# Retention, ELU layer and max-out layer on one core: the planner's stores become steps of their own, ring loads are cut in pieces, buffers change their homes

## The chip, the cores and the metric

The kernel runs on 1 core of a Trainium2 chip. The metric is the device time of one execution in microseconds, lower is better; a program is run several times and the median is given. One further execution was recorded by the profiler; all rows below come from it.

The engines are named as the profile names them: PE is TensorE's matmul, PEld its weight load, DVE VectorE, ACT ScalarE, POOL GpSimd, SP SyncE, which here only issues DMAs. A DMA issue can stand on SP, ACT or POOL, and each of these works through its instructions in the order of the program.

## What is computed

Three stages in a row, all in float32; the weights of stages two and three are stored as float64.

```python
# 1: retention; q, k, v are (4, 8, 768, 64), one decay gamma for each head
for t in range(S):
    state = gamma * state + outer(k[:, :, t], v[:, :, t])
    y[:, :, t] = scale * (q[:, :, t] @ state)
x = y.transpose(0, 2, 1, 3).reshape(3072, 512)
# 2: 512 -> 2048 -> 512 with ELU
h = x @ w_in
x = where(h > 0, h, exp(min(h, 0)) - 1) @ w_out
# 3: 512 -> 768 -> 512, the largest of three products
h = maximum(maximum(x @ w1, x @ w2), x @ w3)
out = h @ w_out2
```

## The kernel before

Float32 values are split into a high and a low part, and three products (high-high, high-low, low-high) stand for one. A matmul has 128 rows, 128 columns and 512 moving columns.

**Stages of work.** The 3072 tokens are six blocks of 512 (`b` 0 to 5). Retention goes by 24 chunks of 128 tokens (`c`), each with scores, a mask, an update of the state and value products. The first chunks and the first products of blocks 0 and 1 are ordered by a list of names (`FIRST`). Then follows the planned part. For blocks 0 to 3 and each of the 16 slices `f` of the inner width there is a first product (`h1_products`, 12 matmuls), the ELU on ACT and DVE (`elu_exp`, `elu_max`, `elu_high`, `elu_low`) and a second product (`o1`, 12 matmuls) that adds into four PSUM banks. Between them stand visits to later chunks (`TURNS` says at which slices). Blocks 4 and 5 are taken together in eight units of seven products of six matmuls (`unit_a`): the operands are sums of quarters of the input and of the weight, so seven products do for eight. The third stage, behind the planned part, uses units of the same kind (`unit`) in a written order.

**Preparation.** The weights of the units are made on the way. `prepare_first` (8 jobs) makes the seven operands of a unit from the split weights of stage two and stores them to `ops_a` in DRAM; `prepare` (12 jobs, `JOBS`; nine with three pairs, three with two) reads float64 words, turns them to float32 in steps on ACT and DVE, forms sums and splits them, and stores the parts to `ops_d`. They use small rings of SBUF buffers: `t` (2), `m` (2), `st` (2 raw words). `prepare_some` adds job `k` to the plan when `(i - BEGIN) * RATE` has passed it, where `i` counts iterations. Where it is added sets which turn in the rings it gets; the planner then decides when it runs.

**The units' ring.** Stored operands come back to SBUF through a ring of three 1 MB buffers of four operands each (`ring`, `fetch`, issued on POOL). A buffer is asked for again when its last operand has been used.

**The planner.** `Plan.add` takes an engine, a cost, a function, and tokens that it reads, writes or comes after. `turn` hands out ring buffers as tokens. `latest` works back from the order of TensorE's steps to the time by which each step is due. `run` plays the plan with the costs: each engine takes, of the steps that are ready, the one that is due first; TensorE may take one of the next six. The functions are then called in the order of the starting times, so each engine's program has that order, and at run time it is kept whatever is late. A store is issued by the function of the step that ends its data (`store`, `store_a`), and a step on the pretended engine Q (`later_read`) holds the buffer for the length of the move. All moves share one queue in the model.

**Partial sums.** `sums_out` and `x2_out` copy the four PSUM banks of a block to SBUF, two on ACT (to `m` buffers) and two on DVE (to `e` buffers, which the ELU uses too), and store them to `x2d`: from ACT's queue, or from POOL's with an addition in DRAM (`again`). Chunks 16 to 23 are stored to `xd` from ACT's queue (`finish_copies`, a buffer of their own, `late_x`). `load_x2("a")` reads `xd` back for the units, and `first_operands` makes the operands of it.

Of the kernel before, what the change touches and what calls it, by code (L numbers as in the profile page):

```python
# [38 lines left out]
TURNS = ((1, 3, 5, 7, 9, 11, 13, 15), (1, 3, 5, 7))  # L39
BEGIN, RATE = 18, 0.31  # L40
# [24 lines left out]
def kernel(ctx: ExitStack, tc: tile.TileContext, qkv0, qkv, wa, wb, dmask, qdec, cols, out):  # L65
# [23 lines left out]
    late_x = ctx.enter_context(tc.tile_pool(name="late_x", bufs=1))  # L89
# [202 lines left out]
    def finish_copies(c):  # L292
        if c >= DEFER:
            x, t0 = late_x.tile([P, NPAIR, P], F32, tag="x", name="xf"), (c - DEFER) * P
            for s in range(2):
                nc.scalar.copy(x[:, :, s * HC:(s + 1) * HC], xo_t[c][s])
            nc.scalar.dma_start(out=xd.rearrange("k p t -> p k t")[:, :, t0:t0 + P], in_=x)
            return
        xh, xl = x_t[c // CB]
        t0 = c * P % BLK  # L300
        xo = xo_t[c]
        for s in range(2):
            nc.scalar.copy(xh[:, :, t0 + s * HC:t0 + (s + 1) * HC], xo[s])

# [236 lines left out]
    def x2_out(b, ms=range(KDM), again=False):  # L541
        for m in ms:
            if b == NB - 1:
                o = (
                    states.rearrange("p b n d -> p (b n d)")[:, m // 2 * BLK:(m // 2 + 1) * BLK] if m % 2 == 0
                    else at.tile([P, BLK], F32, tag=("a", "qd")[m // 2], name="o")
                )
            elif m % 2 == 0:
                o = dpool.tile([P, BLK], F32, tag="m", name="o")
            else:  # L550
                o = gpool.tile([P, BLK], F32, tag="e", name="o", bufs=3)
            to = x2d[m, :, b * BLK:(b + 1) * BLK]
            if m % 2 == 0:
                nc.scalar.copy(o, acc_t[b][m])  # L554
            else:
                nc.vector.tensor_copy(o, acc_t[b][m])
            if again:
                nc.gpsimd.dma_start(out=to, in_=o, accum_op=ALU.add)
            else:
                nc.scalar.dma_start(out=to, in_=o)  # L560
# [4 lines left out]
    class Plan:  # L565
        LAG = {"P": 0.2, "A": 0.06, "D": 0.06, "G": 0.06, "S": 0.06, "Q": 0.0}

        REACH = 6
        FREE = {"P": 0.0, "A": 1.8, "D": 1.4, "G": 0.0, "S": 0.0, "Q": 0.0}
# [4 lines left out]
        def add(self, engine, cost, fn, reads=(), writes=(), after=(), pair=False, move=0.0):  # L574
# [13 lines left out]
            lag = self.LAG[engine] + (move + 3.0 if move else 0.0)  # L588
            self.steps.append((engine, cost, fn, sorted(deps), pair, lag, move))
            return k  # L590

        def turn(self, ring, size):
            n = self.count[ring] = self.count.get(ring, -1) + 1
            return (ring, n), (ring, n - size)

        def latest(self):
# [8 lines left out]
            for _ in range(3):  # L605
                for k in reversed(range(n)):
                    engine, cost, _, _, _, lag, _ = self.steps[k]
                    if engine != "P":
                        ends = [due[u] - lag for u in users[k]]
                        if due[k] is not None:  # L610
                            ends.append(due[k] + cost)
                        due[k] = min(ends, default=clock) - cost
                for engine in "ADG":
                    line = sorted((k for k in range(n) if self.steps[k][0] == engine), key=lambda k: -due[k])
                    end = clock
                    for k in line:
                        due[k] = min(due[k], end - self.steps[k][1])
                        end = due[k]
            return due, users

        def run(self):
            n, due = len(self.steps), None
            due, users = self.latest()
            left, at = [len(x[3]) for x in self.steps], [0.0] * n
# [3 lines left out]
            start, late = [None] * n, 0.0  # L628
            port, queue = [0.0, None], [0.0]
# [4 lines left out]

            def begin(k, t):
                engine, cost, _, _, pair, lag, move = self.steps[k]
                if move:
                    queue[0] = max(queue[0], t + cost + 0.65) + move
                    lag = queue[0] - t - cost + 0.75
# [8 lines left out]
                for u in users[k]:  # L648
                    own = engine == self.steps[u][0] and engine in "P"
                    at[u] = max(at[u], t + cost + (0.0 if own else lag))  # L650
                    left[u] -= 1
                    if not left[u]:
                        known[self.steps[u][0]].append(u)
                        heapq.heappush(times, at[u])

            while len(order) < n:
                assert times, [(k, self.steps[k][0]) for k in range(n) if start[k] is None][:20]
                t = heapq.heappop(times)
                while times and times[0] <= t + 1e-6:
                    heapq.heappop(times)  # L660
                busy = True
                while busy:
                    busy = False
                    for engine in "PSQGAD":
# [11 lines left out]
                        soon = [k for k in known[engine] if at[k] > t + 1e-6]  # L676
                        for k in sorted((k for k in known[engine] if at[k] <= t + 1e-6), key=lambda k: (due[k], k)):
                            end = t + self.steps[k][1]
# [29 lines left out]
    def later_read(*tokens, move=0.77):  # L708
        plan.add("Q", 0.5, None, reads=tokens, writes=(), move=move)

    def prepare_first(p):
# [6 lines left out]
        def whole(i):  # L718
            def fn():
# [3 lines left out]
                for j, n in ((0, 0), (1, 3)) if i == 0 else ((1, 5),):  # L723
                    store_a(slot + n, w[:, :, j * HB:(j + 1) * HB])
# [8 lines left out]
        def third_high():  # L733
            third[0] = dpool.tile([P, 2, HB], F32R, tag="m", name="m")
            nc.scalar.copy(third[0][:, 0], b12())

        def third_low():
            m = third[0]
            nc.vector.tensor_tensor(out=m[:, 1], in0=b12(), in1=f32(m[:, 0]), op=ALU.subtract)
            store_a(slot + 4, m)  # L740
# [4 lines left out]
        def last_low():  # L745
            x = b22()
            nc.vector.tensor_tensor(out=x.bitcast(F32R), in0=x, in1=b12(), op=ALU.subtract)
            store_a(slot + 1, f32(t[1]).rearrange("p (s t) -> p s t", s=2))

        def combined_high():  # L750
            third[1], third[2] = [dpool.tile([P, 2, HB], F32R, tag="m", name="m") for _ in range(2)]
            nc.scalar.copy(third[1], f32(t[0]).rearrange("p (s t) -> p s t", s=2))

        def combined_low():
# [4 lines left out]
            for part, m in enumerate((hi, lo)):  # L759
                stored_a.update((slot + n, part) for n in (2, 6))  # L760
                nc.sync.dma_start(out=ops_a[:, slot + 2:slot + 7:4, part, :], in_=f32(m))

        wait = [("hi", 4 * p), ("lo", 4 * p), ("hi", 4 * p + 2), ("lo", 4 * p + 2)]
        (m0, n0), (m1, n1), (m2, n2) = short("m", 2), short("m", 2), short("m", 2)
# [5 lines left out]
        later_read(wt, ("t", t0), move=1.54)  # L770
        later_read(wt, ("t", t1))
# [6 lines left out]
        plan.add("Q", 0.5, None, [m0], [("prep", p, 0)], move=0.77)  # L778
        add("A", 0.62, combined_high, [A, B_], [m1], [n1, n2])
        add("D", 0.69, combined_low, [A, B_, m1], [m2, t0], [A], True)  # L780
        plan.add("Q", 0.5, None, [m1, m2], [("prep", p, 1)], move=1.54)
        add("A", 0.41, last_high, [D_], [C_])
        add("D", 0.42, last_low, [C_], [D_, t1], (), True)
        plan.add("Q", 0.5, None, [t1, wt], [("prep", p, 2)], move=0.77)

    def prepared(n):
        return [("prep", p, j) for p in sorted({(4 * n + i) // 7 for i in range(4)}) for j in range(3)]

    def prepare(k, slot):
# [20 lines left out]
        def words(i):  # L810
# [27 lines left out]
            add("S", 0.5, load, (), [r], [r0], move=1.54)  # L838
# [5 lines left out]
        def parts(i, key, put):  # L844
            (x, x0), (y, y0) = short("m", 2), short("m", 2)

            def high():
                made[key] = [dpool.tile([P, 512], F32R, tag="m", name="m") for _ in range(2)]
# [177 lines left out]
    def fetch_step(n, reads=(), after=()):  # L1026
        def fn():
            fetch(n)
# [720 lines left out]
```

## Time and profile before

| | us |
|---|---|
| median of 3 runs | 963.96 |
| lowest and highest | 962.66, 966.68 |
| the profiled execution | 970.78 |
| its span, from the first to the last instruction | 968.9 |

The page of the profile gives the busy time of each engine, the chain of work that ended last, and the costliest groups of instructions. A busy time counts an instruction from its start to its end. An idle time is put down to the instruction or DMA that ended it. The stretches that matter here: the list `FIRST` until about 115 us, the planned part until 606 us, and stage three to the end.

### The profile page before, as it was taken

The page shows a single profiled execution, that of the slowest core. Times are in us where ns is not written, and L with a number is a line of the kernel's source. Part 1 is how long each engine was busy: PE and PEld are TensorE (multiplying, and loading weights), DVE is VectorE, ACT ScalarE, POOL GpSimd, SP SyncE. Part 2 cuts the span into 40 slices and gives each one's busy share as a digit, 9 for nine tenths or more (in the row PEclk, how much of TensorE's full clock was granted, in tenths as well). Part 3 has the DMA queues.
Part 4 walks back from the last instruction along what each step waited for, and adds up shares of the span by engine and source line. Part 5 has one row for each costly group of instructions (what it writes and reads, how often), then busy time and mean ns, then how long its engine had stood idle before and what let it go on. Part 6 is the DMA issues. An engine that isn't in the chain of part 4 may idle for free.

```text
span 968.9 us, 16300 instructions
## 1 busy us (share of the span) xinstructions
PE 941.3 (97%) x6583; PEld 770.4 (80%) x6583; DVE 636.4 (66%) x1047; ACT 369.2 (38%) x669; POOL 112.5 (12%) x146
## 2 busy tenths in 40 slices
PE   6999989999999999999998999999999999999998
PEld 4778878877878878887876888888888888888886
DVE  6888678566663346698876888478744787346651
ACT  3566555334443344575654564121220213101111
POOL 2510010214212222000000000100000010000000
PEclk9999999999999999999998999999999999999999
DMA  9934454668763378737776864866525654245602
GB/s 312 327 103 162 136 169 148 144 200 227 229 181 105 110 250 280 235 118 264 242 254 221 280 226 153 303 218 189 191 87 217 194 198 162 98 145 191 206 1 87
DMA packets 86347, 183.26 MB, mean 189 GB/s; under 512 B 6400, under 2 KB 51712, under 8 KB 78336
## 3 DMA queue, kind: packets, MB, share of 16 engines
q1 hardware_dynamic: 67776, 103.83, 32.6%
q0 software_dynamic: 10672, 69.48, 22.6%
q10 hardware_dynamic: 7824, 8.92, 2.7%
q8 instruction: 52, 0.85, 0.4%
q14 instruction: 23, 0.19, 0.1%
HBM read 131.08 MB, written 51.12 MB: 188 GB/s over the span
## 4 chain that ended last, share of the span: by engine, by line
PE 84%; DMA 7%; DVE 4%; ACT 2%; issue 1%; SPq 1%; ACTq 0%; POOL 0%; DVEq 0%; POOLq 0%
PE hp L1163 26%; PE acc L536 18%; PE hp L485 11%; PE acc L1223 10%; PE acc L472 6%; PE hp L462 5%; PE hp L1079 4%; DMA ops_d<-m 2%; DMA ops_a<-t 1%; PE xs L263 1%; PE acc L1163 1%; PE xs L252 1%; PE xs L222 1%; PE xs L194 1%; DMA x<-in_qkv 1%
## 5 line engine op out<-in xcount | busy, mean ns | idle before, releaser
L1163 PE MATMUL hp<-seat,w 128*128 128x512 f32 x1092 | 249.2, 390 | 0.0
L1163 PEld LDWEIGHTS hp<-seat,w 128*128 128x128 f32 x1092 | 204.7, 188 | 43.6 <-ACT states L554 0.4
L536 PE MATMUL acc<-gh,w 128*128 128x512 f32 x600 | 155.9, 399 | 8.5 <-ACT gh L518 8.5
L536 PEld LDWEIGHTS acc<-gh,w 128*128 128x128 f32 x600 | 112.8, 191 | 34.2 <-ACT gh L518 10.2
L485 PE MATMUL hp<-xh,w 128*128 128x512 f32 x376 | 123.7, 390 | 0.0
L1223 PE MATMUL acc<-w,g 128*128 128x512 f32 x432 | 99.1, 389 | 0.0
L1223 PEld LDWEIGHTS acc<-w,g 128*128 128x128 f32 x432 | 81.1, 188 | 16.8
L1079 PE MATMUL hp<-seat,w 128*128 128x512 f32 x336 | 79.7, 395 | 5.3 <-DVE hold L1097 4.6
L536 PE MATMUL acc<-gl,w 128*128 128x512 f32 x300 | 83.8, 393 | 0.4 <-issue 0.4
L485 PEld LDWEIGHTS hp<-xh,w 128*128 128x128 f32 x376 | 70.6, 188 | 14.8
L1079 PEld LDWEIGHTS hp<-seat,w 128*128 128x128 f32 x336 | 63.6, 190 | 19.9 <-DVE hold L1097 5.7
L510 DVE SCALAR_TENSOR_TENSOR e<-e,hp 128x512 f32<-128x512 f32 x59 | 40.5, 686 | 58.1 <-ACT e L504 57.6
L485 PE MATMUL hp<-xl,w 128*128 128x512 f32 x188 | 73.2, 389 | 0.0
L1189 ACT COPY u<-hp 128x512 f32<-128x512 f32 x26 | 15.3, 587 | 138.3 <-PE hp L1163 138.3
L536 PEld LDWEIGHTS acc<-gl,w 128*128 128x128 f32 x300 | 56.7, 190 | 12.8 <-issue 0.8
L503 ACT ACTIVATE e<-hp 128x512 f32<-128x512 f32 x59 | 35.2, 596 | 82.7 <-PE hp L485 68.0
L931 POOL DMA_DIRECT2D w<-ops_d x48 | 25.4, 529 | 355.5 <-PE hp L1163 278.7
L522 DVE TENSOR_TENSOR gl<-e,gh 128x512 fp32r<-128x512 f32 x75 | 53.2, 709 | 14.5 <-ACT gh L518 13.1
L518 ACT CAST gh<-e 128x512 fp32r<-128x512 f32 x75 | 46.4, 619 | 37.4 <-DVE e L510 28.8
L472 PE MATMUL acc<-gh,w 128*128 128x512 f32 x168 | 44.1, 392 | 0.4 <-ACT gh L518 0.4
L171 POOL TENSOR_TENSOR x<-x,cols_sb 128x512 f32<-128x512 f32 x24 | 27.4, 1145 | 137.3 <-DMA x<-in_qkv 137.3
L1180 ACT CAST g<-e 128x512 fp32r<-128x512 f32 x36 | 22.2, 623 | 52.2 <-DVE e L1177 51.8
(146 smaller groups left out, 1294.1 us busy)
## 6 DMA issues: line engine op xcount, KB each, us to landing
w<-ops_d POOLq DMA_DIRECT2D x48, 1024.0 KB, 5.1
x<-in_qkv SPq DMA_DIRECT2D x44, 512.0 KB, 6.4
ops_d<-m SPq DMA_DIRECT2D x66, 256.0 KB, 3.7
raw<-in_wa SPq DMA_DIRECT2D x32, 512.0 KB, 6.1
w<-ops_a POOLq DMA_DIRECT2D x14, 1024.0 KB, 6.8
raw<-in_wb SPq DMA_DIRECT2D x24, 512.0 KB, 4.4
ops_a<-w SPq DMA_DIRECT2D x24, 256.0 KB, 5.2
ops_a<-m SPq DMA_DIRECT2D x24, 256.0 KB, 3.8
```

What stands on the lines that cost most here:

```text
L171: nc.gpsimd.tensor_tensor(out=kd, in0=kd, in1=cols_sb[:, 0:H].rearrange("t (p r) -> t p r", r=2).unsqueeze(3).to_broadcast([P, NPAIR, 2, D ...
L462: nc.tensor.matmul(hp_t[b, f], w_t[0, f // 2][:, f % 2, pw, kk * P:(kk + 1) * P], x_t[b][px][:, kk, :], start=i == 0 and kk == 0, stop=i = ...
L472: nc.tensor.matmul(acc_t[b][m], w_t[1, f // 2][:, f % 2, pw, m * P:(m + 1) * P], g_t[b, f][pg], start=f == f0 and i == 0, stop=f == f1 - 1 ...
L485: nc.tensor.matmul(hp, w[:, pw, kk * P:(kk + 1) * P], x[px][:, kk, :], start=k == 0, stop=k == len(order) - 1,)
L503: nc.scalar.activation(e, hp_t[b, f], ACTF.Exp)
L510: nc.vector.scalar_tensor_tensor(out=e, in0=e, scalar=-1.0, in1=hp_t.pop((b, f)), op0=ALU.mult, op1=ALU.max)
L518: nc.scalar.copy(gh, e_t[b, f])
L522: nc.vector.tensor_tensor(out=gl, in0=e_t.pop((b, f)), in1=f32(gh), op=ALU.subtract)
L536: nc.tensor.matmul(acc_t[b][m], w[:, p[0], m * P:(m + 1) * P], g[p[1]], start=f == f0 and p == first, stop=f == f1 - 1 and p == final, ski ...
L1079: nc.tensor.matmul(ps[name], w[:, pw, kk * P:(kk + 1) * P], x[px][:, kk, :], start=first and k == 0, stop=last and k == 5, skip_group_chec ...
L1163: nc.tensor.matmul(o, w[:, pw, kk * P:(kk + 1) * P], x[px][:, kk, :], start=first and k == 0, stop=last and k == 5, skip_group_check=True,)
L1223: nc.tensor.matmul(acc, g2[f][:, px, m * P:(m + 1) * P], w[:, pw, :], start=f == 0 and i == 0, stop=f == KF2 - 1 and i == 2, skip_group_ch ...
```

## The change

Constants: `TURNS` moves five of twelve visits by one slice, `RATE` goes from 0.31 to 0.5, `OPERANDS` says after which slices of block 3 the steps of `first_operands` are added (all at slice 14 before). The pool `late_x` goes, `m` has three buffers. In the planner, a store is a step on S (SP) or G (POOL); its move is a count and a time of pieces; the two queues are played side by side. A step after a DMA that isn't urgent waits a margin longer, and an issue that isn't due soon is kept back while its queue is full. The visits of chunks 8 to 11 are placed one iteration earlier and the hand-written case of the last of them goes.

```diff
-TURNS = ((1, 3, 5, 7, 9, 11, 13, 15), (1, 3, 5, 7))
-BEGIN, RATE = 18, 0.31
+TURNS = ((1, 3, 5, 7, 9, 11, 13, 14), (2, 4, 6, 8))
+BEGIN, RATE = 18, 0.5
+OPERANDS = (10, 11, 11, 12, 14, 14, 14)
...
-            x, t0 = late_x.tile([P, NPAIR, P], F32, tag="x", name="xf"), (c - DEFER) * P
+            x, t0 = gpool.tile([P, NPAIR, P], F32, tag="e", name="xf", bufs=3), (c - DEFER) * P
...
-            nc.scalar.dma_start(out=xd.rearrange("k p t -> p k t")[:, :, t0:t0 + P], in_=x)
+            late_t[c] = x, xd.rearrange("k p t -> p k t")[:, :, t0:t0 + P]
...
+    def store_late(c):
+        x, to = late_t.pop(c)
+        nc.sync.dma_start(out=to, in_=x)
...
+        elif b < 2 and m % 2 == 0:
+            o = dpool.tile([P, BLK], F32, tag="m", name="o", bufs=3)
+        elif b == NB - 3 and m % 2 == 0:
+            o = at.tile([P, BLK], F32, tag=("a", "qd")[m // 2], name="o")
+        else:
+            o = gpool.tile([P, BLK], F32, tag="e", name="o", bufs=3)
...
+    def x2_store(b, m, o, again=False, eng=nc.sync):
...
+        SLOW = (1.1, 1.5, 1.0, 1.0, 12.0)
...
+        def lag(self, k):
+            engine, cost, _, _, _, move = self.steps[k]
+            return self.LAG[engine] + (3.5 + move[0] * move[1] if move else 0.0)
...
+            def done(k, when, margin):
+                for u in users[k]:
+                    at[u], safe[u] = max(at[u], when(u)), max(safe[u], when(u) + margin)
...
+            def carried(t):
+                while True:
+                    heads = [x[0] for x in lanes.values() if x]
+                    cut = min(t, arrivals[0][0]) if arrivals else t
+                    if heads:
+                        turn = sum(x[2] for x in heads) * self.SLOW[0]
+                        least = min(x[1] for x in heads)
...
+                                        done(x.pop(0)[0], lambda u: clock[0] + 0.75, self.SLOW[1])
...
+                    x = t + (0.8 if engine == "S" else 1.4)
...
+                            if safe[k] > t + 1e-6 and due[k] + late > t + self.SLOW[2]:
+                                continue
+                            if full and self.steps[k][5] and due[k] + late > t + self.SLOW[4]:
+                                continue
...
-    def later_read(*tokens, move=0.77):
-        plan.add("Q", 0.5, None, reads=tokens, writes=(), move=move)
...
+        def put(reads, fn, *made):
+            add("S", 0.42, fn, reads, [("op", slot + n, part) for n, part in made], move=(16, 0.047))
...
-            (x, x0), (y, y0) = short("m", 2), short("m", 2)
+            (x, x0), (y, y0) = short("m", 3), short("m", 3)
...
-                for part, m in enumerate(made[key]):
-                    put(part, m)
...
+            for part, z in enumerate((x, y)):
+                add(
+                    "S", 0.42, lambda part=part: put(part, made[key][part]), [z], [("there", slot, key, part)],
+                    move=(16, 0.047),
+                )
...
-    def fetch_step(n, reads=(), after=()):
+    def fetch_step(n, i, reads=(), after=()):
+        plan.add(
+            "G", 0.6, lambda: fetch(n, i), reads, [("ring", n, i)], list(after) + [("ring", n - RING, i)],
+            move=(10, 0.098),
+        )
...
-            add("S", 0.9, lambda: load(c), (), [raw_of(c)], [raw_of(c - 2)], move=3.1)
+            before = [raw_of(c - 2), kv_of(c - 2)]
+            add("S", 0.42, lambda: load(c, "qk"), (), [raw_of(c)], before, move=(21, 0.098))
+            add("S", 0.42, lambda: load(c, "kv"), (), [kv_of(c)], before, move=(44, 0.052))
...
-            x, x0 = plan.turn("late", 1)
+            x, x0, _ = e_ring()
...
-    for k in range(KF2 // 2):
-        fetch_out(k)
...
+                if x == 0 and 2 <= n < 2 + KF2 // 2:
+                    fetch_out(n - 2)
```

## Rows read from the trace of the kernel before

**Rows 1.** The page, busy time, share of the span, instructions of TensorE.

```profile
PE 941.3 (97%) x6583; PEld 770.4 (80%) x6583; DVE 636.4 (66%) x1047; ACT 369.2 (38%) x669; POOL 112.5 (12%) x146
```

**Rows 2.** Busy time by stage, the planned part: length, engines (count), clock, DMA share, GB/s.

```profile
115.00:606.00 491.00, 476.31 (x3950) 390.23 (x3949) 335.58 (x580) 241.32 (x450) 64.83 (x72) 0.99 0.64 203
```

**Rows 3.** Whom TensorE waited for, 115 to 606 us: total, times, longest.

```profile
PE acc L536 <- ACT gh L518: 8.5, 4, 2.6
PE hp L1079 <- DVE hold L1097: 4.6, 2, 3.6
PE hp L1079 <- DVE e L1042: 0.7, 1, 0.7
```

**Rows 4.** The chain that ended last, pieces in order of time: start, length, what.

```profile
196.46 2.72 PE acc L536 x12
...
202.30 6.29 DMA ops_a<-t
...
211.47 4.61 PE acc L536 x12
...
489.18 8.77 DMA ops_d<-m
...
520.60 2.93 PE hp L1079 x6
523.53 6.79 PE acc L536 x24
```

**Rows 5.** Busy time by stage, behind the last of these waits.

```profile
520.00:540.00 20.00, 19.40 (x74) 15.86 (x75) 14.56 (x26) 8.47 (x15) 1.06 (x2) 0.85 0.62 201
```

**Rows 6.** DMA issues (KB each, median us to landing), and the `ops_d` stores of line 699.

```profile
ops_a<-t SPq DMA_DIRECT2D x8, 256.0 KB, 5.7
...
DMA to landing us min/median/max: 1.7/3.4/8.8
```

**Rows 7.** Busy time by stage of line 852 alone; the timeline of ACT.

```profile
230.00:341.00 111.00, 0.00 (x0) 1.00 0.53 153
341.00:448.00 107.00, 10.34 (x14) 1.00 0.69 225
...
340.54 0.58 ACT L554 COPY o<-acc 128x512 f32<-128x512 f32 x1
```

**Rows 8.** Busy time by stage: PE, PEld, DVE, ACT, POOL, clock, DMA share, GB/s.

```profile
230.00:448.00 218.00, 215.19 (x2356) 176.59 (x2355) 134.26 (x238) 103.78 (x206) 38.74 (x41) 1.00 0.61 188
285.00:341.00 56.00, 56.00 (x738) 46.21 (x742) 21.18 (x40) 20.23 (x44) 11.62 (x12) 1.00 0.37 109
```

**Rows 9.** DVE by line, 135 to 610 us: count, busy us, mean ns, idle before.

```profile
L852 DVE TENSOR_TENSOR m<-t,m 128x512 fp32r<-128x512 f32 x33 | 23.4, 710 | 15.3 <-DMA ops_d<-m 8.5 <-ACT m L849 6.6
L833 DVE SCALAR_TENSOR_TENSOR t<-raw,t 128x512 uint32<-128x512 uint32 x24 | 16.5, 690 | 0.2
...
L808 DVE TENSOR_TENSOR t<-t 128x256 f32<-128x256 f32 x36 | 15.2, 421 | 0.7
```

**Rows 10.** SP's waits, 110 to 140 us; the chain there.

```profile
SPq L122 <- DMA x2d<-o: 8.9, 1, 8.9
...
124.83 7.17 DMA raw<-in_wa
```

**Rows 11.** The ring's loads (line 931): us from issue to landing.

```profile
DMA to landing us min/median/max: 4.4/5.2/10.3
```

**Rows 12.** The timelines of DVE and of POOL at 121 us.

```profile
121.39 1.53 DVE L433 TENSOR_TENSOR w<-t,w 128x512 fp32r<-128x512 f32 x1
...
120.89 1.48 POOL L171 TENSOR_TENSOR x<-x,cols_sb 128x512 f32<-128x512 f32 x1 [63.78 <-DMA x<-in_qkv]
```

**Rows 13.** The timelines of POOL (a chunk's keys) and of TensorE (its scores).

```profile
296.36 1.04 POOL L171 TENSOR_TENSOR x<-x,cols_sb 128x512 f32<-128x512 f32 x1 [4.44 <-DMA x<-in_qkv]
...
301.84 0.58 PE L194 MATMUL xs<-x 64*64 64x64 f32 x28
```

**Rows 14.** SP's waits, 135 to 610 us: total, times, longest.

```profile
SPq L706 <- DVE m L739: 44.8, 6, 17.6
```

More of the change, by code (lines that the diff above doesn't have):

```diff
@@ L572, in __init__, with add @@
             self.steps, self.writer, self.readers, self.count = [], {}, {}, {}
-        def add(self, engine, cost, fn, reads=(), writes=(), after=(), pair=False, move=0.0):
+        def add(self, engine, cost, fn, reads=(), writes=(), after=(), pair=False, move=None):
             k, deps = len(self.steps), set()
@@ L604, in latest @@
                     users[d].append(k)
[L605 to L618, printed above, removed]
+            for k in reversed(range(n)):
+                engine, cost = self.steps[k][:2]
+                if engine != "P":
+                    due[k] = min((due[u] - self.lag(k) for u in users[k]), default=clock) - cost
             return due, users
         def run(self):
-            n, due = len(self.steps), None
+            n = len(self.steps)
             due, users = self.latest()
-            left, at = [len(x[3]) for x in self.steps], [0.0] * n
+            left, at, safe = [len(x[3]) for x in self.steps], [0.0] * n, [0.0] * n
             known = {e: [] for e in "PADGSQ"}
@@ L647, in begin @@
                 heapq.heappush(times, t + cost)
[L648 to L654, printed above, removed]
+                if move:
+                    x = t + (0.8 if engine == "S" else 1.4)
+                    heapq.heappush(arrivals, (x, k))
+                    heapq.heappush(times, x)
+                    return
+                lag = self.LAG[engine]
+                done(k, lambda u: t + cost + (0.0 if engine == self.steps[u][0] == "P" else lag), 0.0)
             while len(order) < n:
@@ L891, in last_low, with last_store @@
             x = b22()
[L892 removed]
             nc.vector.tensor_tensor(out=x.bitcast(F32R), in0=x, in1=b12(), op=ALU.subtract)
[L894 removed]
+        def last_store():
+            stored.update((slot + 1, part) for part in range(2))
+            nc.sync.dma_start(out=ops_d[:, slot + 1], in_=whole(1).rearrange("p (s t) -> p s t", s=2))
         add("A", 0.41, last_high, [D_], [C_])
         add("D", 0.42, last_low, [C_], [D_, ids[1][0]], (), True)
[L898 removed]
+        add("S", 0.42, last_store, [ids[1][0]], [("there", slot, "last", part) for part in range(2)], move=(16, 0.047))
         parts(0, "combined", put_slots(slot + 2, slot + 6))
@@ L1072, in fn @@
             def fn():
-                if pos == 0:
+                if not ps:
                     for x in "abcd":
```

253 lines of the change are left out of this document (137 added, 116 removed).

## The prediction

> **What bounds the kernel now.** I read the page's busy shares first, then the busy time of the planned part, then who TensorE waited for there, then the chain at each of those waits. TensorE is busy 97% of the span [rows 1]; no other engine is above 66% on the page. The change alters no matmul, so it can only win or lose TensorE's idle time and its stretches at the lower clock. Of 968.9 − 941.3 = 27.6 us idle, 491 − 476.3 = 14.7 lie between 115 and 606 us [rows 2], where the planner sets the order; the rest belongs to the opening, whose order is a written list, and to the end, and I leave it alone. The reader should see in [rows 3] that TensorE waits in the planned part almost only for ACT's `gh` (8.5 us in 4 waits, 2.6 of it at 132 us, so 5.9 at 206, 222 and 282 us) and for DVE's `hold` (4.6 us, at 498 and 517 us), both steps of the activation. And in [rows 4], what held these up: DVE, which takes its instructions in order, stood before a preparation step whose buffer a store had not yet left (`ops_a<-t` 6.3 us, `ops_d<-m` 8.8 us; there are two such pieces of each kind), and the activation stood behind it.
>
> After two of these waits TensorE's granted clock falls from 2.4 to 1.2 GHz for a while (mean 0.85 of full in 520 to 540 us [rows 5], the engine having waited in two places before). Its price is read from groups of matmuls at either level [rows 4]: 12 take 2.72 us at full clock, 0.227 each. At 211 us 12 take 4.61, so 1.9 us more; at 520 us 6 take 2.93 for 1.36 and 24 take 6.79 for 5.44, so 2.9 more. That is 4.8 us of clock beside 14.7 of idle: 19.5 us, the most that the plan could give.
>
> **The change part by part, against the profiled span of 968.9 us.** (That execution took 970.78 us; the median of the three timed runs is 963.96, 4.9 below the span. I subtract the same gain from both.)
>
> *Stores as steps, a third `m`.* Today a store is issued inside the DVE step that ends its data, and a Q step stands for its landing. In the new plan each store has an S step of its own, the queues share the wire, the buffer's next user depends on the landing, and a step that isn't urgent waits 1.5 us longer (`SLOW`). This bears on the waits at 206 and 222 us (idle and 1.9 of clock), at 282 us (the preparation's `t` there waits for something that the profile doesn't name, most likely the `t` buffer again) and at 498 and 517 us (4.6 idle and 2.9 of clock). Against it: the model lets a 256 KB store land 0.8 + 16 × 0.047 × 1.1 + 0.75 = 2.4 us after its issue, 3.9 with the margin, and the trace has medians of 3.4 and 5.7 us, with 8.8 at worst [rows 6]. So the margin covers about the ordinary store and not those that hurt, which is why I don't book all of it.
>
> *Other homes for partial sums.* The copy of block 2's sums takes `m` buffers today, and its turns were handed out ahead of the second weight set's. So `L852`, the writer of `m` for that set, runs nowhere from 230 to 341 us and begins right behind that copy at 340.5 us [rows 7]; in 285 to 341 us DVE is 38% busy and the DMA engines 37% [rows 8]. The change takes `m` for blocks 0 and 1 only and adds jobs faster (`RATE` 0.5 for 0.31), so this hole can be filled. A job with three pairs costs DVE at most 2 × 3 × 0.690 + 3 × 0.710 + 5 × 0.421 = 8.4 us (two conversions, three `m`, five half-width steps [rows 9]), one with two pairs 5.6: 9 × 8.4 + 3 × 5.6 = 92 us. 14 of the 33 `m` writes, so some 39 us, come before 448 us today [rows 7]. DVE's idle time in 230 to 448 us is 218 − 134.3 = 83.7 us [rows 8], so the other 53 fit, at 86% busy. Then the waits at 498 and 517 us, among the units, lose their cause and are not only planned better, and this raises the share that I book.
>
> *Loads.* The wait at 132 us comes from SP. A chunk load holds it for 8.9 us, since its buffer still feeds `x2d<-o`; the weight half behind it is issued at 124.8 us and takes 7.2 us to land, and ACT stands before it ahead of an exponential [rows 10]. No step of the plan, old or new, knows of that buffer. The new rule keeps a load that isn't due within 12 us back while its queue holds over 1 us, which may or may not put the weight half first. Between 0 and 2.6 us I take the middle, 1.3; no row is nearer to one end.
>
> *ACT's stores go to SP.* Twelve stores of sums and eight of late rows leave ACT's sequencer, which is 38% busy and waits mostly for others: 0 there. SP takes 20 issues more; their cover and price are in the last rival. The wait of 0.7 us at 456 us (an `e` buffer that `x2d<-o` holds) is now modelled, and the even stores of block 3 move to `a` and `qd`.
>
> *Late rows in the `e` ring.* Eight chunk outputs borrow one of three `e` buffers until their store has landed. Two iterations of 5.4 us (24 matmuls of 0.227) lie between such visits and take one `e` each, so the buffer is asked for again after 11 us or more, against 8.8 at worst [rows 6]: 0. If the cover is gone it costs 0.7, as the `e` wait at 456 us did [rows 3], four times at most: 0 to 2.8, and I take 0.7.
>
> *Ring in pieces.* The 17 loads of 1 MB in the planned part become 68 of 256 KB, so 51 more issues on POOL (12% busy). A piece is asked for 12 products of 6 matmuls ahead, so at least 72 × 0.227 = 16 us, against 10.3 us for the slowest whole megabyte [rows 11]: 0, and if that cover were gone, 10.3 − 8.8 = 1.5 us a time. What pieces do to the stores is a rival's business.
>
> *The rest.* `fetch_out` moves behind the first units of the last part, where TensorE doesn't idle and the weights are wanted only once nine units are done: 0. `TURNS` moves the last chunk, and with it the late rows, one iteration: 5.4 us later. TensorE never waits for these operands today [rows 3]: 0, or up to 5.4 us once if there was no cover at all; 0 taken. `OPERANDS` only hands out the same steps earlier: 0.
>
> *Sum.* 5.9 + 1.9 (206 to 282 us) + 0.7 (456) + 4.6 + 2.9 (498, 517) = 16.0 us. I book three quarters, 12.0, as the margin covers the median landing but not the worst, and 1.3 at 132 us. Against it stand 0.7 for `e` and 2 for waits at new places (preparation packed to 86% busy will stand before ELU again once, at about the size of one wait in [rows 3]). Gain 10.6, say 11 us: span 958, **median 953 us**.
>
> **The rivals.** *Nearly all goes.* If the landing model holds, DVE never stands before a buffer while an activation is due. For it: the hole, which gives time. Against it: landings of 8.8 us. Gain 18 of 19.5 us, 946. Chance 0.2.
>
> *The stalls move with the preparation.* In 230 to 448 us POOL works for 38.7 us [rows 8], and DVE steps that meet it stretch: `w` at 121.39 us took 1.53 us beside POOL's 1.48, against 0.71 for its like [rows 9, 12]. If all of POOL's time were lost to DVE, its 83.7 free microseconds would become 45 for 53 of preparation; jobs would stay among the units, DVE would have no slack, and the four waits would come back elsewhere: gain 0 to 2, about 963. The Trainium skill (GPSIMD Engine Reference, Key points) says that GpSimd contends with VectorE instructions that read two SBUF inputs, as these do; the trace agrees in that pair. The Trainium skill (DMA: Bandwidth & Descriptors, Rules for kernel authors) also asks for 1 MiB or more per DMA, against the pieces; by that rule stores would land later beside them, and no row here shows it. Chance 0.19.
>
> *SP becomes the line in which all wait: slower.* SP issues in order, and each chunk load would stand among more stores that wait for ACT and DVE. One chunk's keys are done at 297.4 us and its products begin at 301.8: 4.4 us of cover [rows 13]. SP waited 44.8 us in 6 waits for `m L739` alone, 7.5 each [rows 14]. If half of the 16 planned chunks met such a wait, each would be 7.5 − 4.4 = 3.1 us late and cost about 1 more of clock: 33 us, against 17 won, 980. It decides from the point where a store ahead of a chunk load waits over 4.4 us. Against it: such waits exist today, and no chunk load makes TensorE wait in the planned part [rows 3]. Chance 0.11.
>
> **How the numbers follow.** The forecast has 0.5: 953, its own range 947 to 959. Eight in ten, with the first two rivals, lie in 944.5 to 967. About 0.5% (4.8 us, below 959.1) is what a measurement of this kernel can tell from no change. Faster by more: 0.48 of the forecast, 0.2, and 0.04 of the moved stalls, 0.72; within: 0.17; slower: 0.11.
>
> **What would show it.** Right: `L852` runs between 285 and 341 us; DVE's waits for `ops_a` and `ops_d` stores fall to less than half; TensorE's idle time in the planned part is 3 to 7 us, and the clock reads 1.00 in 520 to 540 us. Wrong: TensorE waiting for `x<-in_qkv` or for POOL's keys (the SP rival), or for `gh` behind DVE waits of the old total at 240 to 440 us (the moved stalls), or a time above 967.

## The result, and the profile after

| | before | after |
|---|---|---|
| median, us | 964.02 (4 runs) | 952.87 (4 runs) |
| lowest and highest | 962.66, 966.68 | 952.43, 953.54 |
| the profiled execution, its span | 970.78, 968.9 | 953.54, 951.8 |

The ratio is 0.988, with an interval of 0.986 to 0.990. The forecast was 953. Between the two profiled executions, though, lie 17.1 us of span, not 11, and a good part of what follows is about that difference. One execution of the kernel before in the series below, at 974.63 us, counts as a slow one and is left out of the ranges.

First the page of after, the busy time of TensorE and the others, then its windows of 115 to 606 us and of 520 to 540 us (columns as in [rows 2]):

```profile
PE 936.9 (98%) x6583; PEld 768.5 (81%) x6583; DVE 642.8 (68%) x1047; ACT 369.2 (39%) x669; POOL 143.1 (15%) x197
```

```profile
115.00:606.00 491.00, 488.73 (x4026) 401.53 (x4025) 347.00 (x589) 244.25 (x455) 95.52 (x125) 1.00 0.68 210
520.00:540.00 20.00, 20.00 (x90) 16.57 (x89) 16.45 (x28) 11.43 (x21) 5.30 (x10) 1.00 0.84 265
```

TensorE's idle time in the planned part falls from 14.7 us [rows 2] to 2.3, so by 12.4. Its busy time over the whole span falls from 941.3 [rows 1] to 936.9, so by 4.4: the same matmuls, less of them at the lower clock, and 520 to 540 us reads 1.00 for 0.85 [rows 5]. 0.3 of idle time went elsewhere. 12.4 + 4.4 + 0.3 = 17.1: the account between the two traces is closed.

What TensorE still waits for there, all of it; DVE's waits for stores in that stretch before (three rows), and its only one after:

```profile
PE acc L542 <- ACT gh L524: 1.1, 1, 1.1
PE hp L491 <- DVE xl L320: 0.8, 1, 0.8
PE xs L252 <- ACT cols_sb L276: 0.3, 1, 0.3
```

```profile
DVE m L852 <- DMA ops_d<-m: 8.5, 6, 2.0
DVE m L756 <- DMA ops_a<-m: 8.3, 5, 3.9
DVE t L722 <- DMA ops_a<-t: 8.2, 2, 4.5
```

```profile
DVE t L764 <- DMA ops_a<-t: 3.1, 1, 3.1
```

Every wait of [rows 3] is gone. The `gh` wait of 1.1 us lies at a new place, `xl` is new, and the one for `cols_sb` was there before with the same 0.3 us. The pieces of [rows 4] in which a store held DVE have no successor that TensorE feels. DVE waited 25 us for such stores before, 3.1 now. (The lines have moved: L518 is L524, L536 is L542, L485 is L491, L852 is L901.)

The 1.1 us lie at 125.7 us. The timelines of DVE and of POOL just before:

```profile
120.80 1.41 DVE L412 SCALAR_TENSOR_TENSOR t<-raw,t 128x512 int32<-128x512 int32 x1
122.14 1.78 DVE L439 TENSOR_TENSOR w<-t,w 128x512 fp32r<-128x512 f32 x1
125.20 0.69 DVE L439 TENSOR_TENSOR w<-t,w 128x512 fp32r<-128x512 f32 x1
```

```profile
120.59 1.08 POOL L171 TENSOR_TENSOR x<-x,cols_sb 128x512 f32<-128x512 f32 x1 [62.94 <-DMA x<-in_qkv]
121.92 1.45 POOL L181 TENSOR_TENSOR qd<-x,qdec_sb 128x512 f32<-128x512 f32 x1 [0.25 <-DMA x<-in_qkv]
```

Two DVE steps of 0.69 us took 1.41 and 1.78 while POOL worked, and in the chain ACT's `gh` stands behind them. The `w` step on the third line, with POOL idle, took 0.69.

### The profile page after: what moved, and what is told of

Same layout as the page of the kernel before. It is cut to its first block, busy times and chain, and to the rows that moved or that the text cites. A ratio compares the mean times of both kernels' runs of the same rounds, so it can differ in the third digit from the quotient of the medians.

```text
span 951.8 us, 16453 instructions
## 1 busy us (share of the span) xinstructions
PE 936.9 (98%) x6583; PEld 768.5 (81%) x6583; DVE 642.8 (68%) x1047; ACT 369.2 (39%) x669; POOL 143.1 (15%) x197
## 4 chain that ended last, share of the span: by engine, by line
PE 95%; DVE 3%; DMA 1%; ACT 1%; ACTq 0%; issue 0%; SPq 0%
PE hp L1215 26%; PE acc L542 21%; PE hp L491 13%; PE acc L1275 10%; PE hp L1134 8%; PE acc L478 6%; PE hp L468 4%; PE xs L263 1%; PE xs L252 1%; PE acc L1215 1%; PE xs L194 1%; PE xs L222 1%; DMA x<-in_qkv 1%; DVE t L412 1%; PE sc L329 0%; DVE t L418 0%
## 5 line engine op out<-in xcount | busy, mean ns | idle before, releaser
L542 PE MATMUL acc<-gh,w 128*128 128x512 f32 x600 | 153.5, 393 | 1.1 <-ACT gh L524 1.1
L542 PEld LDWEIGHTS acc<-gh,w 128*128 128x128 f32 x600 | 110.9, 188 | 25.5 <-ACT gh L524 2.2
L491 PE MATMUL hp<-xh,w 128*128 128x512 f32 x376 | 123.2, 389 | 0.8 <-DVE xl L320 0.8
L491 PEld LDWEIGHTS hp<-xh,w 128*128 128x128 f32 x376 | 70.6, 188 | 15.9 <-DVE xl L320 1.2
L542 PE MATMUL acc<-gl,w 128*128 128x512 f32 x300 | 83.1, 390 | 0.0
L985 POOL DMA_DIRECT2D w<-ops_d x57 | 30.2, 529 | 350.5 <-PE hp L1215 278.5
L491 PE MATMUL hp<-xl,w 128*128 128x512 f32 x188 | 73.2, 389 | 0.0
L542 PEld LDWEIGHTS acc<-gl,w 128*128 128x128 f32 x300 | 56.2, 188 | 11.9
L524 ACT CAST gh<-e 128x512 fp32r<-128x512 f32 x75 | 46.4, 619 | 25.8 <-DVE e L516 18.4
L985 POOL DMA_DIRECT2D w<-ops_a x56 | 29.9, 537 | 131.5 <-PE hp L1134 110.9
L478 PE MATMUL acc<-gh,w 128*128 128x512 f32 x168 | 44.4, 394 | 1.1 <-ACT gh L524 1.0
```

Source lines behind the costliest of these rows:

```text
L478: nc.tensor.matmul(acc_t[b][m], w_t[1, f // 2][:, f % 2, pw, m * P:(m + 1) * P], g_t[b, f][pg], start=f == f0 and i == 0, stop=f == f1 - 1 ...
L491: nc.tensor.matmul(hp, w[:, pw, kk * P:(kk + 1) * P], x[px][:, kk, :], start=k == 0, stop=k == len(order) - 1,)
L524: nc.scalar.copy(gh, e_t[b, f])
L542: nc.tensor.matmul(acc_t[b][m], w[:, p[0], m * P:(m + 1) * P], g[p[1]], start=f == f0 and p == first, stop=f == f1 - 1 and p == final, ski ...
L985: nc.gpsimd.dma_start(out=ring[n % RING][:, a:z].rearrange("p s h t -> p (s h t)"), in_=src[:, 4 * k + a:4 * k + z].rearrange("p s h t -> ...
```

## The experiments

Each was timed beside the kernel before on the same chip; ratios are against it, with their interval. The kernel before scatters: its single executions in these series lie between 957.65 and 969.69 us, up to 10 or 11 us apart on one chip, its medians between 962.25 and 964.02. The four executions of the kernel after lie within 1.1 us. In the experiments that start from the kernel before the update step also comes after its scores, as in the kernel after, so that each order that the plan finds is a possible one; the planner's order of the kernel before is the same with and without this. A difference of one or two microseconds from the kernel after (952.87) compares runs of different series and is said with that reserve.

### Is it the hole, and the room that it gives?

The reason that I gave for booking the stalls at 498 and 517 us was that block 2's sums, out of `m`, let preparation run in the hole at 285 to 341 us [rows 7]. The first run makes that change alone in the kernel before.

```diff
-            if m % 2 == 0:
+            if m % 2 == 0 and b != 2:
                 x, x0 = plan.turn("m", 2)
```

> The kernel before, with one part of the change: the even sums of block 2 go to e buffers instead of m. Two theories of where the 11 us came from. Hole: the preparation of the second weight set was held up from 230 to 341 us by the turns in m, and so stood among the units; then L852 runs in 285 to 341 us here, the two waits at 498 and 517 us (4.6 us, and the clock behind them) go, and the time is 956 to 959 us. Landing: it is only the longer time the new planner allows a store; then the waits come back at other places, and the time is 962 to 966 us.

Measured: 970.31 us, ratio 1.009 (1.006 to 1.012), slower. Line 852 alone, by stage (DVE busy, count, clock, DMA share, GB/s):

```profile
285.00:341.00 56.00, 5.51 (x8) 1.00 0.71 221
341.00:395.00 54.00, 4.13 (x6) 1.00 0.89 284
395.00:450.00 55.00, 0.00 (x0) 1.00 0.20 66
450.00:500.00 50.00, 3.44 (x5) 0.93 0.67 210
```

The hole is filled, and another opens at 395 to 450 us, ahead of block 3's sums, whose turns in `m` are handed out in the same way. TensorE waits 10.7 us for `gh` where it waited 8.5.

Perhaps the room is only of use with jobs added faster. The same kernel with `RATE` 0.5:

```diff
-BEGIN, RATE = 18, 0.31
+BEGIN, RATE = 18, 0.5
```

> The kernel before with its own planner, block 2's even sums in e buffers and the rate of jobs 0.5 for 0.31 (with the old rate the hole only moved to 395 to 450 us, behind the sums of block 3). Room: the preparation now runs ahead of the units without a hole, DVE has time left, and 952 to 958 us follow. Planner: the old planner still sets steps on DVE and ACT ahead of stores that land late, the waits for ops_a and ops_d stores stay at 20 us or more, and 962 to 972 us follow.

Measured: 1017.03, ratio 1.057 (1.052 to 1.063). TensorE waits 18.0 us for `gl` and 12.0 for `gh`; ACT's `m` step waits 18.3 us for `ops_d` stores in nine places, for 11.7 in five before. The theory of the hole falls: in this planner, room and rate make it worse.

The other way round, the kernel after with block 2's even sums back in `m`, and all else kept:

```diff
-        elif b < 2 and m % 2 == 0:
+        elif b < 3 and m % 2 == 0:
...
-            if b < 2 and m % 2 == 0:
+            if b < 3 and m % 2 == 0:
```

> The changed kernel with the even sums of block 2 back in m buffers. Hole: the preparation of the second weight set waits for these sums again, runs into the units, and TensorE idles there; 956 to 960 us. Landing: the planner allows for the stores wherever the preparation stands; 952 to 954 us.

Measured: 964.81, ratio 1.001 (0.999 to 1.004). The whole gain is gone, so the home does matter: TensorE's idle time in the planned part is 8.8 us, and its busy time over the span is 6.3 us above the kernel after (clock). But not by a hole. Line 901 by stage, of this run and (second fence) of the kernel after, and TensorE's longest wait in this run:

```profile
230.00:285.00 55.00, 5.60 (x6) 0.94 0.78 232
285.00:341.00 56.00, 6.64 (x9) 1.00 0.76 249
```

```profile
230.00:285.00 55.00, 2.27 (x3) 1.00 0.70 218
285.00:341.00 56.00, 5.15 (x7) 1.00 0.70 226
```

```profile
PE hp L491 <- DVE xl L320: 4.3, 1, 4.3
```

With the old home 15 writes of `m` fall between 230 and 341 us, in the kernel after 10. It is crowded, not empty. The steps that crowd are seen in the chain (the first fence), in DVE and in POOL:

```profile
227.95 7.97 DMA x2d<-o
...
243.59 4.92 DMA ops_a<-w
```

```profile
244.96 3.50 DVE L769 TENSOR_TENSOR t<-t 128x256 f32<-128x256 f32 x4
```

```profile
244.34 1.73 POOL L181 TENSOR_TENSOR qd<-x,qdec_sb 128x512 f32<-128x512 f32 x1
246.04 1.22 POOL L171 TENSOR_TENSOR x<-x,cols_sb 128x512 f32<-128x512 f32 x1
```

A sum store with addition takes 7.97 us to land, where the plan allows 1.4 + 8 × 0.2 × 1.1 + 0.75 = 3.9 for one that has the queues to itself; ACT's exponential waits 2.2 us for its `e` buffer. Then four half-width steps of 0.42 us take 3.50 beside POOL, the `ops_a<-w` store lands at 248.5 us, and `xl` stands behind both. A likely reason for the crowding lies in the code: a job whose turn in `m` is ahead of the copy's must be done before the copy, and the copy is due when the block ends. With jobs added at 0.5 there are more of them. This is read from the code and the counts; no run isolated it, and the old home with the old rate was not tried.

### Is it the landing of the stores?

In the kernel before, the allowance for a landing is made 2.5 us longer, and nothing else.

```diff
-                    lag = queue[0] - t - cost + 0.75
+                    lag = queue[0] - t - cost + 3.25
```

> The kernel before, with its planner's landing time of every move 2.5 us longer (0.75 becomes 3.25), buffers and homes as before. Landing: DVE's waits for stores fall from 25 us to under 8, TensorE's idle time in the planned part falls from 14.7 to under 6, 951 to 956 us. Hole: the preparation is still packed among the units, where DVE has no room, 960 to 965 us.

Measured: 980.62, ratio 1.019 (1.015 to 1.023). Slower by some 17 us, and yet the old stalls are gone: TensorE's waits for `gh` add up to 1.5 us for 8.5, and none lies at 498 or 517 us. In their place stand two others. What TensorE waited for (the first line from 115 to 606 us, the second behind it), and lines of DVE's timeline at the first:

```profile
PE hp L1079 <- DVE hold L1097: 10.5, 1, 10.5
```

```profile
PE acc L1163 <- ACT o L554: 6.2, 1, 6.2
```

```profile
449.86 0.68 DVE L556 COPY o<-acc 128x512 f32<-128x512 f32 x1
458.12 0.69 DVE L556 COPY o<-acc 128x512 f32<-128x512 f32 x1 [7.58 <-DMA x2d<-o]
...
459.33 0.69 DVE L522 TENSOR_TENSOR gl<-e,gh 128x512 fp32r<-128x512 f32 x1
...
460.45 0.69 DVE L522 TENSOR_TENSOR gl<-e,gh 128x512 fp32r<-128x512 f32 x1
```

DVE waited 7.58 us to copy the second of block 3's two sums in `e`, until the first one, stored from ACT's queue, had landed in `x2d`. So the allowance cures what I had read in [rows 4], and block 3's sums, of which I had costed the new homes and the move to SP at next to nothing, then cost 10.5 us. The 6.2 are another matter: ACT's copies of block 4's sums wait for `m` buffers that `ops_d` stores of the preparation hold, which now ends later.

By the code, the 7.58 us are not an allowance too short. These stores have it too (`later_read` in `sums_out`), but the planner gives the two sums two buffers and sets their copies right behind each other. Two of the ELU's `e` buffers are still to be read then, by the two `gl` steps behind the copies, so of three only one is left. That the second copy therefore got the first one's buffer is read from this order and the code. It fits the other runs: two `gl` steps stand behind the copies with the new due times alone (6.12 us of waiting) and in the next run (1.59 us, stored from SP), while in the kernels before and after it is one, and nothing waits.

Both together, in the old planner: the longer allowance, the new homes (block 2 in `e`, block 3 in `a` and `qd`) and the sums stored from SP.

```diff
+                    lag = queue[0] - t - cost + 3.25
...
-            if m % 2 == 0:
+            if b < 2 and m % 2 == 0:
                 x, x0 = plan.turn("m", 2)
+            elif b == NB - 3 and m % 2 == 0:
+                x, x0 = plan.turn(("a", "qd")[m // 2], 1)
...
-                nc.scalar.dma_start(out=to, in_=o)
+                (nc.scalar if b == NB - 1 else nc.sync).dma_start(out=to, in_=o)
```

> The kernel before with three small edits together: the 2.5 us longer allowance for a store's landing in the old model, the new homes of the even block sums (block 2 in e, block 3 in a and qd), and the stores of block sums issued from SP instead of ACT's queue. Theory: what carries the gain is that the order allows for the landing, together with homes that no slow store holds; steps of their own, margin, due times and queues played side by side are not needed. Then the 10.5 us wait behind block 3's sums goes, TensorE's idle time from 115 to 606 us is below 5 us, and the time is 950 to 958. Rival: the stores have to be steps, since only then does the order know when SP and the wire reach them; then waits of 5 us or more stay at block 3's or the last blocks' sums and the time is 962 or more, as with the longer allowance alone (980.6). Rival two: with preparation held back by the longer allowance the rows of block 3's sums and the units still meet; the time then lies between, 958 to 970, with gh or hold named as what TensorE waits for at 450 to 610 us.

Measured: 961.77 over ten executions, all within 960.02 to 963.14; ratio 0.998 (0.996 to 1.000). The planned part, and TensorE's longest wait behind it:

```profile
115.00:606.00 491.00, 486.90 (x4009) 398.39 (x4008) 345.40 (x588) 242.31 (x454) 70.37 (x76) 1.00 0.65 207
```

```profile
PE hp L1165 <- DMA w<-ops_d: 3.1, 1, 3.1
```

Some 19 us better than the allowance alone: the 10.5 and the 6.2 are gone, and idle time in the planned part is 4.1 us for 14.7. So allowance and sums together cure the stalls of the plan, and the scatter of the kernel before with them. But the time is 8.9 above after. On the traces (spans 959.9 and 951.8) 1.8 of the 8.1 are idle time in the plan, 3.0 idle time behind it, where an operand load of stage three comes late, and 3.0 TensorE's busy time (939.9 for 936.9), so clock. That a time in between would come was the second rival; the wait that it named, `gh` or `hold`, was the wrong one. What the homes and what the move to SP bring of the 19 us was not taken apart. What lies behind the plan here, POOL's issues first, then the chain (the last line for a like stretch at full clock):

```profile
599.20 1.20 POOL L942 DMA_DIRECT2D w<-ops_d  x2
600.57 0.53 POOL L942 DMA_DIRECT2D w<-ops_d  x1 [0.17 <-issue]
```

```profile
607.06 13.41 DMA w<-ops_d
...
620.61 65.88 PE hp L1165 x282
...
738.17 66.72 PE hp L1165 x294
```

The late load took 13.41 us to land, behind the three megabytes of `fetch_out` (line 942), which the change moves behind the first units; in the kernel after no such wait is left. The 282 matmuls after it take 1.9 us more than at the rate of the 294. So by this estimate some 5 of the 8.1 us lie at this place, and `fetch_out`, which I had put at 0, is the nearest cause. No run moved it alone.

The opposite, the kernel after with a landing that costs nothing beyond the issue:

```diff
-        SLOW = (1.1, 1.5, 1.0, 1.0, 12.0)
+        SLOW = (0.0, 0.0, 1.0, 1.0, 12.0)
...
-    done(x.pop(0)[0], lambda u: clock[0] + 0.75, self.SLOW[1])
+    done(x.pop(0)[0], lambda u: clock[0], self.SLOW[1])
...
-                    x = t + (0.8 if engine == "S" else 1.4)
+                    x = t + cost
```

> The changed kernel with a planner for which every move lands the moment it is issued (no time on the wire, none before and behind it; the dues keep theirs). Landing: DVE and ACT are set before buffers that are not free, their waits for stores come back to 20 us or more, and 960 us or more follow. Dues: the steps that can stand are due late and come late anyway; 952 to 957 us.

Measured: 1048.55, ratio 1.089 (1.083 to 1.094). TensorE's largest wait, DVE's for the two kinds of stores, all from 115 to 606 us:

```profile
PE acc L542 <- ACT gh L524: 45.8, 16, 5.8
```

```profile
DVE m L901 <- DMA ops_d<-m: 11.8, 5, 3.8
DVE t L764 <- DMA ops_a<-t: 11.8, 4, 4.3
```

All the other parts of the change were in this kernel, and it is 96 us slower than after. So an order without landings undoes all the rest. But it takes away more than the change brought, since the kernel before has landings in its model too (one queue, 0.65 and 0.75 us beside each move, loads included). What the new model of them is worth against the old one, no run shows by itself.

### What carries nothing

The margin of 1.5 us, on which I had made the booked share depend, set to zero:

```diff
-        SLOW = (1.1, 1.5, 1.0, 1.0, 12.0)
+        SLOW = (1.1, 0.0, 1.0, 1.0, 12.0)
```

> The changed kernel without the margin of 1.5 us behind a landing. Landing: DVE's waits for stores come back to 10 us or more and TensorE's idle time in the planned part to 6 us or more, 956 to 960 us. Hole: the preparation has room, so a late store meets no activation; 952 to 954 us.

Measured: 953.24, and the kernel after is at 952.87. DVE waits 1.4 us for stores to `ops_a` and `ops_d`. The margin carries nothing of the time.

The old rate in the new planner:

```diff
-BEGIN, RATE = 18, 0.5
+BEGIN, RATE = 18, 0.31
```

> The changed kernel with the old rate of 0.31. With the new homes only blocks 0 and 1 share m with the preparation, so the rate sets no more than which jobs come ahead of their sums. Room: 953 to 956 us, L901 still runs in 285 to 341 us. If the rate itself carries the gain: 958 to 964 us, and the preparation runs later into the units.

Measured: 951.14, all four executions within 950.86 to 951.42. TensorE is idle 0.6 us in the planned part. The rate isn't needed for the gain. Whether it costs the 1.7 us between the two is open: the ratio is 0.988 for both.

Two `m` buffers for three (every `bufs=3` of `m` and its turns):

```diff
-            (x, x0), (y, y0) = short("m", 3), short("m", 3)
+            (x, x0), (y, y0) = short("m", 2), short("m", 2)
```

> The changed kernel with two m buffers instead of three. Room: a pair needs both, so the next pair waits for a landing, the preparation gets slower by a third and ends among the units, 955 to 960 us. Planner: it waits where it harms nobody, 952 to 954 us.

Measured: 951.77. The third buffer carries nothing.

The ring's loads whole, 1 MB each, in the new planner:

```diff
-            "G", 0.6, lambda: fetch(n, i), reads, [("ring", n, i)], list(after) + [("ring", n - RING, i)],
-            move=(10, 0.098),
+            "G", 0.6, lambda: fetch(n), wait[n], [("ring", n, k) for k in range(4)],
+            list(after) + [("ring", n - RING, k) for k in range(4)], move=(40, 0.098),
```

> The changed kernel with the ring's loads in whole megabytes again, issued once the last of four operands is used. If the pieces are free and gain nothing: 952 to 954 us. If whole megabytes delay the stores beside them (stores of 256 KB land at 5 us or more by median between 450 and 550 us): 955 to 958 us.

Measured: 952.90. Pieces or whole, the time is the same. The `ops_d<-m` stores beside them between 450 and 550 us land in 4.0 us by median, with pieces in 4.5: if anything later beside the pieces, as the second rival had it, and at no cost.

One part of the diff I had not costed at all: `latest`, which lost its three passes that keep an engine's due times apart. The old passes in the new planner, and the new function in the old:

```diff
-            for k in reversed(range(n)):
-                engine, cost = self.steps[k][:2]
-                if engine != "P":
-                    due[k] = min((due[u] - self.lag(k) for u in users[k]), default=clock) - cost
+            for _ in range(3):
+                ...
+                for engine in "ADG":
+                    ...
+                        due[k] = min(due[k], end - self.steps[k][1])
```

> The changed kernel with the old way to work out due times (three passes that also push the steps of one engine apart, so that preparation is due earlier than its users ask). Neither margin, rate, third m nor ring pieces carried the gain. Dues: with the old ones preparation goes ahead of activations, TensorE waits for gl and gh as in the run with home and rate on the kernel before; 970 us or more. Landing: the new planner knows when a store lands, whatever the dues; 951 to 956 us.

Measured: 950.52 (949.70 to 951.35), ratio 0.988 (0.984 to 0.992). That is 2.3 us below after, in another series and at the same ratio; TensorE's idle time in the planned part is 0.8 us for 2.3.

> The kernel before with the new, plain due times and nothing else. Dues: activations go first, the waits for gh behind preparation go, TensorE's idle time in the planned part falls from about 13 to 6 us or less; 952 to 957 us. Landing: DVE still stands before buffers that the planner takes for free; 960 to 966 us.

Measured: 968.91, ratio 1.006 (1.004 to 1.009), slower. TensorE's idle time in the planned part is 12.6 us, and 5.6 of it stand behind block 3's second copy in `e`:

```profile
453.51 0.69 DVE L556 COPY o<-acc 128x512 f32<-128x512 f32 x1 [6.12 <-DMA x2d<-o]
```

The due times aren't the gain either.

## Why the prediction was right, and where it was not

**What bounds the kernel: right.** Idle time in the planned part and the clock were nearly the whole of it; the clock's term of 4.8 us came out at 4.4, the idle term of 14.7 gave 12.4.

**Three quarters of 16.0 us: the step that failed, by its size and by what it was set against.** All the waits that make up the 16.0 went on the traces, not three quarters of them. The profiled execution of before is 6.8 us above the median of its runs, and its span was the one the sum started from. "I subtract the same gain from both" is the sentence that was wrong: the executions of the kernel before differ by up to 13 us (957.65 to the profiled 970.78), and the sum was read off the dearest of them. From this trace 17.1 us were won, from the median 11.15. That the dear execution had more stalls than the others is likely but not shown, since it is the only trace of that kernel; the profiled execution is also the slowest of its series in 7 of 13 kernels, so some of the 6.8 us may belong to profiling. The two errors cancelled. That the forecast of the median was 0.13 us off is luck and not the working.

**Why the share was three quarters: wrong.** I set the margin against the worst landing [rows 6]. The margin carries nothing (953.24 without it). An order that puts the next use of a buffer behind the ordinary landing is needed (without any landing 1048.55); that the queue played with its load is what does it better than the old model is argued, not shown. Whether steps of their own are needed is open: the old model with a fixed longer allowance, new homes and SP reaches 4.1 us of idle time in the plan, but 961.8, and much of the rest lies at the loads of `fetch_out`.

**Other homes: the effect underrated, the reason wrong.** I put them down as room for preparation. Filling the hole by itself costs 7 us (970.31 against 963.19); room with rate costs 55 (1017.03 against 962.25). Without the new home of block 2 all of the gain goes, most likely by crowding ahead of the copy, and without the homes and SP for the sums the longer allowance stalls for 10.5 and 6.2 us. Preparation left the units in part only: line 901 still runs in 450 to 550 us, 12 times for 13 before, and once for 6 times in 550 to 606 us. "ACT's stores go to SP: 0" was argued from ACT's load and left out the buffer behind the store: where two sums share one, the second copy waits for the landing. The 12 stores of blocks 2 to 4 land in 2.2 us by median from SP in the kernel after:

```profile
x2d<-o SPq DMA_DIRECT2D x12, 256.0 KB, 2.2
```

From ACT's queue before it was 5.0 us. But the queue is not shown to be the reason: the last four of the 12 landed in 2.0 us from ACT's queue before, and block 2's four took 5.8 from SP with allowance and homes in the old planner.

**Loads, 1.3: about right.** The wait of 2.6 us at 132 us is gone; the chunk's load no longer stands ahead of the weight half [rows 10]. The 1.1 us at 125.7 that came for it has another cause, by the chain DVE beside POOL: 1.5 gained.

**Late rows in `e` (0.7), new waits (2): too dear.** No TensorE wait for an `e` buffer is left, and the new waits are `xl` with 0.8 and, counted under loads, `gh` with 1.1. **Ring in pieces (0):** right, the 51 more issues on POOL included: POOL's busy time grew by 30.6 us, and whole loads give the same time. The third `m`, which I had named beside the stores' steps, carries nothing. `TURNS`, `OPERANDS` and `fetch_out` were not tried alone. Their zeros have no run behind them, and for `fetch_out` the trace with allowance and homes speaks against it.

**The rivals.** *Nearly all goes* described the traces (17.1 of 19.5), though its 946 started from the wrong execution. *The stalls move with the preparation* had a true mechanism at a small price: DVE steps stretched beside POOL cost 1.1 us in the kernel after, and they carry part of the loss in the kernel with the old home. *SP becomes the line:* SP does wait more, as expected, and by waits above the 4.4 us from which I let it decide; its largest row from 135 to 610 us, beside [rows 14]:

```profile
SPq L744 <- ACT m L898: 71.2, 22, 16.8
```

But no chunk load made TensorE wait in the planned part. A wait of SP isn't a late load as long as the plan has placed the load ahead of it.

**The signs.** Of the four for "right", three came: line 901 runs between 285 and 341 us (7 times), DVE's waits for stores fell to an eighth, the clock reads 1.00. TensorE's idle time, 2.3 us, is below the 3 to 7 that I had named. The first of them should not have stood as a sign: with the old home line 901 runs there 9 times, and the gain is gone.

## What to carry to other kernels

When an order is fixed ahead and kept at run time, the time by which a store's buffer may be used again must be in the model, and so must the buffer that a step will really get: here a longer allowance cured the old stalls, and two sums that the plan had given two buffers then waited for each other. Take a sum of stalls from several executions, or set it against the median's own trace, since one trace can be several microseconds dearer than the median. The old due times (950.5 us) or the old rate (951.1) serve as well as the change itself, with less idle time in their traces; at one ratio, 0.988, none of the three is shown to be the best, and both together were not run.

## What was not expected of the hardware

The kernel before scatters by up to 10 or 11 us from one execution to the next on one chip, with one program. Others stay closer: 0.6 us (old rate, four executions), 1.1 (the kernel after, four), 3.1 (allowance and homes in the old planner, ten), 2.3 (old home in the new planner, ten). That this comes of landings is not shown: the kernel without any landing in its model stays within 3.5 us (four).

How long one kind of store takes to land depends on its place. Of the 12 `x2d<-o` stores of blocks 2 to 4, 256 KB each from ACT's queue, the last four landed in 2.0 us by median before and the eight others in 5.6. With addition, from POOL's queue, the median was 6.7 us after.

A DVE step with two SBUF inputs of 0.42 us took up to 1.40 (line 769 with the old home) and one of 0.69 took 1.78, so 1.0 to 1.1 us more, beside instructions of POOL of 1.73 and 1.45 us, which take 1.28 at the least in these two kernels. The Trainium skill (SBUF — State Buffer, Who interferes with whom) says that a DVE instruction with two SBUF inputs contends with a GpSimd one that reads SBUF, and that the shared port pair is an exclusive lock. The trace agrees: in these places the loss is no more than one POOL instruction, and nothing is lost when POOL is idle (0.69 at 125.20 us).
